# Sending the crossbar's q transpose two slots sooner in an attention and feed-forward kernel

The kernel runs on **one core of one Trainium2 chip**. The metric is the device time of one execution in microseconds (us), lower is better; medians of several runs are given with their range.

## The reference

```python
scale  = 1.0 / np.sqrt(64)                          # q, k, v: (8, 8, 576, 64) float32
scores = scale * np.matmul(q, k.transpose(0, 1, 3, 2))
thresh = np.max(scores, axis=-1, keepdims=True) - tau        # tau = 0.02
scores = np.where(scores >= thresh, scores, -1e9)
attn   = softmax(scores)                            # max taken off, sum + 1e-9
x = np.matmul(attn, v).transpose(0, 2, 1, 3).reshape(4608, 512)
h = x @ w_in                                        # 512 x 2048
y = (h - np.tanh(h)) @ w_out                        # 2048 x 512
```

## The kernel before

The 64 heads are handled as 32 **pairs**, 0 to 31. Each pair has nine score tiles; one tile is one **slot** of the schedule, and the scores run AHEAD = 8 slots in front of the rest. I write 9.5 for tile 5 of pair 9. Between the slots the program does the feed-forward layers of batches that are ready, so TensorE has work nearly all the time. The profiler's short names are used below: PE for TensorE's matmuls, PEld for its weight loads, DVE for VectorE, ACT for ScalarE, POOL for GpSimd, SPq for the sync engine's queue; L370 is line 370 of the kernel.

What a pair needs before its first tile is planned in slots ahead of it (cut to what matters):

```python
raw_pool = pool("raw", 2); hl_pool = pool("hl", 2); qk_pool = pool("qk", 2)
z_pool = pool("z", 4); zt_pool = pool("zt", 6); p_pool = pool("p", 3)

PREP = (
    (LDK, lambda p: load(p, "k")),          # LDK = 16; two DMAs each, sync queue
    (LDK - 1, lambda p: load(p, "q")),
    (LDK - 2, lambda p: load(p, "v")),
    (8, lambda p: split(p, "k")),           # GpSimd: float32 -> two fp16 halves
    (7, lambda p: split(p, "q")),
    (5, lambda p: turn(p, "k")),            # PE transposes, DVE copy
    (4, split_v),
)
for p in range(1, NPAIR):
    first = TPP * p - AHEAD
    for d, f in PREP[3 if p == 1 else 0 :]:
        d -= p == 1 and d in (3, 5)
        if d == 5 and p >= 5:
            d = 6 if p % 2 else 3
        plan.setdefault(first - d, []).append(lambda p=p, f=f: f(p))
    d = 5 if q_by_dma(p) else (2) if p >= 5 else 3 - (p == 1)
    plan.setdefault(first - d, []).append(lambda p=p: turn(p, "q"))
```

In 13 pairs (9, 11, ... 29, and 30 and 31) q is turned by the DMA crossbar, on the sync engine's queue; in the others by nine PE transposes and a DVE copy:

```python
def q_by_dma(p):
    return p >= 2 * HPAIR and (p % 2 == 1 or p == 30)

def turn(p, t):
    hl = hls.pop((p, t))
    if t == "q" and q_by_dma(p):
        m = mats[p, t] = qk_pool.tile([P, W], FP16, name=f"{t}T", tag=t)
        nc.sync.dma_start_transpose(out=..., in_=...)        # L247, qT<-qhl
        return
    ... # PE transposes to ps_q (L235), then nc.vector.tensor_copy (L258)
```

The same queue carries all loads, the output stores and 117 other transposes, one for most pairs of score tiles: ACT writes z, the crossbar turns it into zT, ACT takes the exponential of it (pT), and PE multiplies pT by v.

```python
def kink(i):        # ACT: z (L363)
    ...
        zts[i] = zt_pool.tile([P, TPP, P], BF16, name="zT")
        nc.sync.dma_start_transpose(out=zts[i], in_=zt)      # L370, zT<-z
def weights(i):     # ACT: pT = exp(zT) (L399); PE then uses pT (L420, L427)
```

## Time and profile before

| | before |
|---|---|
| median of 3 runs | 535.39 us (534.58 to 536.02) |
| profiled run | 536.14 us, span 534.4 us, granted clock 1.0 |

The prediction shows the engine table, the stretch from 100 to 440 us, the waits and one stall. Four more views are needed later. First pair 9, as the windows view has it from 115 to 130 us (its columns are window, length, busy us of PE, PEld, DVE, ACT, POOL, clock, DMA share and GB/s). ACT is busy 14.44 of 15 us here, against 307 of 340 over the whole stage:

```profile
115.00:130.00 15.00, 14.04 (x145) 7.91 (x142) 12.86 (x40) 14.44 (x20) 9.05 (x14) 1.00 1.02 201
```

### The profile page before, as it was taken

To read this page: it belongs to the slowest core of one execution; us is meant where nothing else is said; L and a number is where in the kernel's file an instruction comes from. 1 tells how busy PE (TensorE), PEld (TensorE's weight loads), DVE (VectorE), ACT (ScalarE), POOL (GpSimd) and SP (SyncE) were. 2 spreads that over 40 slices of the span, in tenths; PEclk is the share of its full clock that TensorE was granted. 3 is DMA by queue.
4 is the path that set the end of the run, shared out by engine and by line. 5 is a ranking of instruction groups with operands and counts; after the bars stand their busy time and mean duration, and the time that the engine had idled before them with its cause. 6 is when DMAs were issued, how large, how long until landed. Compare 5 with 4: busy or idle time off the path is not lost.

```text
span 534.4 us, 12822 instructions
## 1 busy us (share of the span) xinstructions
PE 509.6 (95%) x4651; PEld 289.2 (54%) x4651; DVE 423.3 (79%) x1184; ACT 436.7 (82%) x617; POOL 289.5 (54%) x390
## 2 busy tenths in 40 slices
PE   8988899999999998989999999999999999999997
PEld 4666566555555554555555555655555555444444
DVE  5888878989989897889889898899889887554440
ACT  5999899999898988899888989899889999543330
POOL 7999987775737566574727474575747530000000
PEclk9999999999999999999999999999999999999999
DMA  7655547999996999799998999798988995401113
GB/s 203 183 186 146 182 151 186 211 163 200 173 201 146 173 189 201 151 182 195 173 199 140 213 165 210 153 188 185 207 167 178 204 148 110 104 20 41 39 40 79
DMA packets 202687, 85.32 MB, mean 160 GB/s; under 512 B 170240, under 2 KB 195072, under 8 KB 202624
## 3 DMA queue, kind: packets, MB, share of 16 engines
q1 hardware_dynamic: 202032, 84.08, 75.2%
q8 instruction: 36, 0.59, 0.5%
q10 hardware_dynamic: 592, 0.43, 0.3%
q14 instruction: 27, 0.22, 0.1%
HBM read 36.70 MB, written 9.44 MB: 86 GB/s over the span
## 4 chain that ended last, share of the span: by engine, by line
PE 64%; DVE 9%; POOL 9%; DMA 7%; ACT 6%; issue 4%; SPq 0%; POOLq 0%; ACTq 0%; DVEq 0%
PE psY L519 20%; PE psH L493 16%; PE psS L326 14%; DMA qT<-qhl 5%; PE psO L427 3%; PE psHt L493 3%; DVE sc L336 3%; DVE g L512 2%; ACT z L363 2%; POOL kS L264 2%; PE psS L317 2%; DVE yo L532 2%; PE ps_k L235 2%; ACT th L506 1%; POOL w_in_sb L626 1%
## 5 line engine op out<-in xcount | busy, mean ns | idle before, releaser
L336 DVE TENSOR_SCALAR_CACHE_REDUCE sc<-psS 128x576 f32<-128x576 f32 x288 | 214.3, 752 | 40.7 <-PE psS L326 22.0
L363 ACT ACTIVATE z<-sc,nb 128x576 bf16<-128x576 f32 x288 | 217.2, 770 | 32.5 <-DVE nb L348 30.2
L519 PE MATMUL psY<-w_out_sb,g 128*128 128x512 bf16 (+1 forms) x592 | 145.9, 374 | 0.8 <-DVE yo L532 0.8
L264 POOL COPY kS<-kT 64x1152 f16<-64x1152 f16 x62 | 70.8, 1142 | 126.3 <-DVE nb L348 124.7
L399 ACT ACTIVATE pT<-zT 128x1152 f16<-128x1152 bf16 x117 | 135.0, 1154 | 2.0 <-DMA zT<-z 2.0
L493 PE MATMUL psH<-xT,w_in_sb 128*128 128x512 bf16 x480 | 123.3, 379 | 2.3 <-DVE g L512 2.3
L326 PE MATMUL psS<-kT,qT 128*128 128x512 f16 (+1 forms) x512 | 104.4, 285 | 4.6 <-DVE qT L258 1.2
L326 PEld LDWEIGHTS <-qT 128*128 128x128 f16 x1024 | 74.2, 97 | 59.2 <-issue 5.1
L512 DVE SCALAR_TENSOR_TENSOR g<-th,psH 128x512 bf16<-128x512 f32 x128 | 87.4, 683 | 18.9 <-ACT th L506 18.6
L326 PE MATMUL psS<-kS,qT 128*128 128x512 f16 x496 | 101.4, 286 | 0.0
L506 ACT ACTIVATE th<-psH 128x512 f32<-128x512 f32 x128 | 74.7, 583 | 23.7 <-PE psH L493 23.0
L519 PEld LDWEIGHTS <-g 128*128 128x128 bf16 x592 | 51.0, 98 | 56.8 <-issue 2.4
L493 PEld LDWEIGHTS <-w_in_sb 128*128 128x128 bf16 x576 | 49.1, 98 | 57.0 <-issue 4.7
L427 PE MATMUL psO<-vb,pT 128*128 128x65 bf16 x1024 | 53.3, 194 | 0.0
L427 PEld LDWEIGHTS <-pT 128*128 128x128 f16 x1024 | 44.2, 98 | 9.7
L188 POOL TENSOR_TENSOR qhl<-qraw,qhl 128x576 f16<-128x576 f32 x31 | 39.7, 1280 | 2.6
L188 POOL TENSOR_TENSOR khl<-kraw,khl 128x576 f16<-128x576 f32 x31 | 39.7, 1280 | 2.6
L391 ACT ACTIVATE pT<-psZ 128x512 f16<-128x512 bf16 (+1 forms) x54 | 35.0, 651 | 5.0 <-PE psZ L382 4.5
L532 DVE COPY yo<-psY 128x512 f32<-128x512 f32 (+1 forms) x31 | 21.1, 681 | 14.1 <-PE psY L519 12.4
L453 DVE TENSOR_TENSOR osb<-psO,rc 128x256 bf16<-128x256 f32 x64 | 27.1, 424 | 2.2
L420 PE MATMUL psO<-vb,pT 128*128 128x130 bf16 x128 | 28.2, 220 | 0.4
L258 DVE COPY kT<-ps_k 128x1152 f16<-128x1152 f16 x31 | 23.3, 752 | 5.8 <-PE ps_k L235 5.8
(79 smaller groups left out, 516.9 us busy)
## 6 DMA issues: line engine op xcount, KB each, us to landing
vraw<-in_v_dram SPq DMA_DIRECT2D x32, 256.0 KB, 3.7
out_dram<-yo SPq DMA_DIRECT2D x32, 256.0 KB, 3.1
kraw<-in_k_dram SPq DMA_DIRECT2D x31, 256.0 KB, 3.6
qraw<-in_q_dram SPq DMA_DIRECT2D x31, 256.0 KB, 3.7
wt<-in_moe_w_in_dram SPq DMA_DIRECT2D x8, 512.0 KB, 4.7
wt<-in_moe_w_out_dram SPq DMA_DIRECT2D x8, 512.0 KB, 4.4
zT<-z SPq DMA_TRANSPOSE x117, 3.5
kraw<-in_k_dram SPq DMA_DIRECT2D x32, 32.0 KB, 3.5
```

The lines of the kernel that those rows point to most:

```text
L188: nc.gpsimd.tensor_tensor(out=hl[:, :, 1, :], in0=x, in1=hl[:, :, 0, :], op=ALU.subtract)
L264: nc.gpsimd.tensor_copy(out=o, in_=i)
L326: nc.tensor.matmul(out=ps[:, dst], lhsT=lhs, rhs=kk[:, src], start=(n == 0), stop=(n == 1),)
L336: nc.vector.tensor_scalar(out=sc, in0=ps[:, lo : lo + S], scalar1=SC, scalar2=None, op0=ALU.mult, op1=ALU.max, accum_out=mx[:, c : c + 1],)
L363: nc.scalar.activation(out=z, in_=sc, func=ACT.Prelu, bias=nb, scale=1.0, alpha=STEEP)
L391: nc.scalar.activation(out=pt[:, off * P : (off + n) * P], in_=ps[:, 0 : n * P], func=ACT.Exp)
L399: nc.scalar.activation(out=pt[:, 0 : n * P], in_=zts.pop(i)[:, 0:n, :], func=ACT.Exp)
L427: nc.tensor.matmul(out=po[:, t - 1 + ab, :], lhsT=pt[:, blk * P : (blk + 1) * P], rhs=vb[:, hh, c, :], start=False, stop=(n == 7), skip_gr ...
L493: nc.tensor.matmul(out=ps, lhsT=w_in_sb[:, c, n * P : (n + 1) * P], rhs=xs[m][:, c, :] if m < B else xR[:, c, :, :], start=(c == 0), stop= ...
L506: nc.scalar.activation(out=th, in_=ps, func=ACT.Tanh)
L512: nc.vector.scalar_tensor_tensor(out=gs[m][:, n, :], in0=th, scalar=-1.0, in1=ps, op0=ALU.mult, op1=ALU.add,)
L519: nc.tensor.matmul(out=ps, lhsT=gs[m][:, n, ms * P : (ms + 1) * P], rhs=w_out_sb[:, n, cols], start=(n == 0), stop=(n == DF_C - 1),)
```

## The change

The intent: the q transpose leaves the queue earlier, so that PE need not wait for it at the first tile of a pair. For that GpSimd's split of k and q is planned two slots sooner too. And pairs 2 and 4, still turned by PE, turn q one slot later.

```diff
@@ -654,10 +654,12 @@
         for d, f in PREP[3 if p == 1 else 0 :]:
             d -= p == 1 and d in (3, 5)
+            if d in (7, 8) and q_by_dma(p):
+                d = d + 2
             if d == 5 and p >= 5:
                 d = 6 if p % 2 else 3
             plan.setdefault(first - d, []).append(lambda p=p, f=f: f(p))
-        d = 5 if q_by_dma(p) else (2) if p >= 5 else 3 - (p == 1)
+        d = 7 if q_by_dma(p) else 3 - (p == 1 or p % 2 == 0 or p >= 5)
         plan.setdefault(first - d, []).append(lambda p=p: turn(p, "q"))
```

## The prediction

> **What bounds the kernel now.** I read the page's engine table first, then the stretch in which attention and the two feed-forward layers run together, then the list of waits, then the chain of waits, then the timeline around one stall. The engine table, and the busy time of each engine from 100 to 440 us (columns: window, length, busy us of PE, PEld, DVE, ACT, POOL with instruction counts, clock, DMA share, GB/s):
>
> ```profile
> PE 509.6 (95%) x4651; PEld 289.2 (54%) x4651; DVE 423.3 (79%) x1184; ACT 436.7 (82%) x617; POOL 289.5 (54%) x390
> ```
>
> ```profile
> 100.00:440.00 340.00, 331.53 (x3070) 187.05 (x3067) 297.97 (x847) 306.97 (x413) 201.59 (x259) 1.00 0.94 180
> ```
>
> TensorE is busy 331.5 of 340 us there; ACT has 10% to spare, DVE 12%, POOL 41%, and the clock is granted in full. So only something that idles PE can be won: at most 340 - 331.5 = 8.5 us by that row. The last 70 us are feed-forward layers alone, which the change does not touch. What idles PE is in the list of waits (engine, line, what it waited for: us in total, times, longest):
>
> ```profile
> PEld L317 <- DMA qT<-qhl: 7.3, 8, 1.7
> ...
> PE psS L317 <- DMA qT<-qhl: 3.4, 3, 1.4
> ...
> PEld L326 <- DMA qT<-qhl: 1.0, 1, 1.0
> ...
> PE psS L326 <- DMA qT<-qhl: 0.9, 1, 0.9
> ```
>
> The greatest wait of PE by far is for the crossbar-turned q of a new pair. The matmul rows are the same events as some of the weight rows, seen one pipeline stage later, so they must not be added. The chain of waits around 231 us (start, length, what):
>
> ```profile
> 230.60 0.06 POOL kS L264
> 230.66 1.06 issue
> 231.72 5.72 DMA qT<-qhl
> 237.44 0.04 issue
> 237.48 0.69 PE psS L317 x8
> ```
>
> The transfer sent at 231.72 lands at 237.44 and PE goes on 0.04 us later. The timeline of the same stretch shows why it was sent no sooner (start, length, instruction):
>
> ```profile
> 226.13 1.30 SPq L370 DMA_TRANSPOSE zT<-z  x1
> ...
> 226.38 1.28 POOL L188 TENSOR_TENSOR qhl<-qraw,qhl 128x576 f16<-128x576 f32 x1
> ...
> 227.53 0.53 SPq L145 DMA_DIRECT2D kraw<-in_k_dram  x1
> ...
> 230.35 1.26 SPq L370 DMA_TRANSPOSE zT<-z  x1
> ...
> 231.72 2.02 SPq L247 DMA_TRANSPOSE qT<-qhl  x1
> ...
> 237.48 0.39 PEld L317 LDWEIGHTS <-qT 128*64 128x64 f16 x8 [1.73 <-DMA qT<-qhl]
> ```
>
> GpSimd had the split q ready at 226.38 + 1.28 = 227.66, 4.1 us before the transfer left. Between the two the sync queue sent four loads and a zT, because the program puts them ahead.
>
> **What the skill says.** (1) The Trainium skill, "Perfetto Trace Analysis", section "Per-instruction lifecycle: what the profiler-reported window actually captures": a hardware-queue DMA's slice covers the issuing and not the movement. The trace agrees: the issue at 231.72 took 2.02 us, its landing 5.72 us. So I take landings from the chain and from semaphores. (2) "DMA: Bandwidth & Descriptors", section "Queues, rings and completion order": all DMAs of the sync engine share one ring on each of the 16 DMA engines, consumed in ring order. Sending q sooner therefore makes what it overtakes later. The trace agrees in kind: in the back-to-back stretch from 227.53 us zT took 6.2 us to land, against 3.5 in the median. (3) The first page's section "Identifying the Most-Contended Engine" calls matmul busy time a bad measure of headroom because matmuls are pipelined. Here PEld is at 54% while PE is at 95%, so I size the gain from the gaps in front of single weight loads, not from the 95%.
>
> **The change part by part.** The order of instructions on each engine, compared between the two builds, shows how little really moves.
>
> Splitting two slots sooner: GpSimd's sequence is identical in both kernels, so this part only lets the sync queue's instruction follow in program order. Gain by itself: 0.
>
> Sending two slots sooner: 13 transfers (pairs 9, 11, ... 29, and 30, 31). In the usual case one jumps over four loads, sometimes an output store, and one zT. From transfer to transfer (231.72, 260.49, 290.69) two pairs, 18 slots, take about 29 us, so a slot is 1.62 us and two are 3.2 us. It can use nearly all of that: by the trace the split was ready 3.9 to 5.9 us before the old issue in all 13 cases. In the new place the sync queue reaches the transfer within about 0.2 us of the split's end (227.48 against 227.66 in the case shown; the same offset in most pairs), so the queue hardly blocks. The longest wait, 1.73 us, is less than 3.2 us: all these waits should vanish.
>
> Size: the weight-load rows give 7.3 + 1.0 = 8.3 us in 9 events. A load after such a change of tile costs some 0.23 us in any case (the timeline shows [0.23 <-issue] in front of the next group at 238.10), so 9 x 0.23 = 2.1 us stays, and 6.2 us goes. Taking the excess of start-to-start distances of matmuls over their usual distance I get 6.2 us too, in seven pairs (9, 15, 17, 19, 21, 30 at 0.3 to 1.6 us each, one negligible); in the other six q came in time already. Nearly all of it is on the path, as PE sets the pace of this stage.
>
> Given back: the zT that is overtaken leaves one transposing issue later (1.3 to 2.7 us). Most of these zT lie ready 1.6 to 3.4 us before ACT reads them, but in pairs 9, 15 and 17 only 1.24, 0.58 and 0.66 us. I count 1 us of ACT waiting in each of these three, 3 us, and a third of it passed on to PE, since ACT has 10% to spare and the result is used two slots later: 1 us.
>
> Pairs 2 and 4 turn q (nine PE transposes) one tile later, and the DVE copy of 0.75 us moves behind the next bias. There the list of waits has PE waiting for DVE's qT copy 1.2 us in 2 events; in those stretches ACT runs without a gap, so the wait is mostly not the path. I count 0, give or take 0.3 us.
>
> Sum: 535.4 - 6.2 + 1.0 = **530.2 us**, 1.0% faster.
>
> **The rivals.** (a) *The wait moves to zT.* If the crossbar, not the place in the queue, is scarce (DMA share 0.94 over this stage), the overtaken zT land where q landed before, ACT waits in more pairs, and th and z behind it are late. For it: landings of 6.2 us when two transposes queue behind four loads, and a zT with a slack of 0.1 us right after the transfer in four pairs. Against it: ACT waited for zT only 2.0 us (4 times) in all, and zT's median slack is 3.2 us. It would give back 3 to 6 us: 532 to 535. (b) *ACT or DVE becomes the bound.* PE's stalls let ACT catch up; in some 15 us windows ACT is busy 14.8. With the stalls gone ACT's share rises from 307/340 to 307/334 = 92%, so a lasting bound is unlikely, but PE may wait more for g and for psS. It would leave 2 to 3 us of gain: 532 to 533. (c) *The sync queue blocks.* If GpSimd is late, the transfer holds up zT and loads behind it. The split is ready within 0.2 us in most pairs (0.6 in pair 9), and loads are sent a whole pair ahead, so this costs under 0.5 us. (d) *More than the stalls.* If a stall also delays the chain behind it (DVE waited 1.35 us at 238.21 for the same q), removing it gains no more than PE lost; 8.5 us is the ceiling: 527.
>
> **Range and chances.** The sum gives 530.2. Rivals (a) and (b) pull towards 533, the ceiling towards 528; runs before spread from 534.6 to 536.0. I take 528.2 to 533.4 as 8 in 10. Faster by over 2% means under 524.7, more than the whole idle time of PE in the stage: 2%. Slower by over 2% would need the sync queue to jam: 1%. Within 2%: 97%.
>
> **What would show it.** Right: the waits of PE and PEld for DMA qT fall from 8.3 us to under 1; q is sent about 3 us sooner (near 228 in the case shown) and lands before 234; PE's idle time from 100 to 440 us falls by about 5 us; GpSimd's busy time stays. The give-back is seen in ACT's wait for zT: 2.0 us now, 3 to 5 expected. Wrong: PEld still waits for qT (then the DMA, not the place in the queue, is slow); ACT pT waiting for zT beyond 6 us with new PE waits for pT or g (rival a); PE idle as before with DVE or ACT as the releasers (rival b); the sync queue waiting long for GpSimd's qhl (rival c).

## More of the kernel before

Third, the waits of ACT for zT and of PE for pT (total, times, longest), both small:

```profile
ACT pT L399 <- DMA zT<-z: 2.0, 4, 0.9
...
PEld L420 <- ACT pT L399: 1.3, 3, 0.4
```

Fourth, a line of the queue table that looks like nothing (packets, MB, share). It is TensorE's instruction stream, in 36 packets of 16,384 bytes; one such packet is called a fetch below:

```profile
q8 instruction: 36, 0.59, 0.5%
```

Second, the sync queue's timeline in pair 9 (start, length, instruction). The four loads of k and q have gone out by 114.4; then come a zT, the q transpose, the v loads and three zT:

```profile
114.44 1.84 SPq L370 DMA_TRANSPOSE zT<-z  x1
116.46 1.31 SPq L247 DMA_TRANSPOSE qT<-qhl  x1
117.83 0.62 SPq L145 DMA_DIRECT2D vraw<-in_v_dram  x1
118.49 0.66 SPq L151 DMA_DIRECT2D vraw<-in_v_dram  x1
119.25 4.40 SPq L370 DMA_TRANSPOSE zT<-z  x3
```

## The result

| | before | after |
|---|---|---|
| median, range | 535.62 us, 534.58 to 536.02 (4 runs) | **533.94 us**, 533.65 to 534.50 (4 runs) |
| ratio | | 0.9973, 95% interval 0.9956 to 0.9990 |
| profiled run, span | 536.14, 534.4 us | 534.50, 532.5 us |

All these runs are at clock 1.0. A ratio is the mean time of one kernel's fast runs over the mean of the other's of the same rounds, so it is not quite the ratio of the medians. The change is real and small: about 1.5 us of the 5.2 predicted, and outside the predicted range.

**The wait that was to go is gone.** In the list of waits of the kernel after, no line has PE or PEld waiting for DMA qT; before they were 8.3 us. The case that the prediction shows, near 231 us, reads now (sync queue):

```profile
226.16 1.30 SPq L370 DMA_TRANSPOSE zT<-z  x1
227.73 1.30 SPq L247 DMA_TRANSPOSE qT<-qhl  x1
229.09 0.58 SPq L145 DMA_DIRECT2D kraw<-in_k_dram  x1
...
231.59 1.84 SPq L370 DMA_TRANSPOSE zT<-z  x1
```

The transfer leaves at 227.73 instead of 231.72 and lands at 230.97. PE first loads from it at 235.89, in the second half of the 16 loads of L317 that begin at 235.40.

**Other waits have grown.** The list of waits of the kernel after, for the same two pairs of names as above, with one new line (PE for pT) and what the sync queue itself waited for GpSimd:

```profile
PEld L420 <- ACT pT L399: 4.5, 8, 1.0
...
ACT pT L399 <- DMA zT<-z: 3.7, 6, 1.4
...
PE psO L420 <- ACT pT L399: 1.1, 2, 0.6
```

```profile
SPq L247 <- POOL qhl L188: 2.3, 10, 0.5
```

ACT waits 1.7 us more for zT and PE's weight loads 3.2 us more for pT. ACT's longest such waits after are 1.48 us in two pieces in pair 9, where there was none before, and 1.45 near 425 us (0.46 before). The timeline of pair 9 shows how it comes about. The q transpose now goes ahead of the four loads. The zT, which stands behind the loads as before, leaves at 116.91 instead of 114.44:

```profile
113.06 1.28 SPq L247 DMA_TRANSPOSE qT<-qhl  x1
114.39 0.58 SPq L145 DMA_DIRECT2D kraw<-in_k_dram  x1
115.02 0.56 SPq L153 DMA_DIRECT2D kraw<-in_k_dram  x1
115.63 0.59 SPq L145 DMA_DIRECT2D qraw<-in_q_dram  x1
116.27 0.55 SPq L153 DMA_DIRECT2D qraw<-in_q_dram  x1
116.91 1.83 SPq L370 DMA_TRANSPOSE zT<-z  x1
118.79 0.59 SPq L145 DMA_DIRECT2D vraw<-in_v_dram  x1
119.43 0.65 SPq L151 DMA_DIRECT2D vraw<-in_v_dram  x1
120.18 5.03 SPq L370 DMA_TRANSPOSE zT<-z  x3
```

The queue issues without a pause for 12 us. ACT and PE in the same stretch (brackets: idle time before, and what ended it):

```profile
120.95 1.16 ACT L399 ACTIVATE pT<-zT 128x1152 f16<-128x1152 bf16 x1 [0.50 <-DMA zT<-z]
...
122.17 0.10 PEld L420 LDWEIGHTS <-pT 128*128 128x128 f16 x1 [0.76 <-ACT pT L399]
...
124.43 1.16 ACT L399 ACTIVATE pT<-zT 128x1152 f16<-128x1152 bf16 x1 [0.98 <-DMA zT<-z]
...
125.64 0.10 PEld L420 LDWEIGHTS <-pT 128*128 128x128 f16 x1 [0.53 <-ACT pT L399]
```

Two zT come late in a row, and PE waits after each of them. In the chain of waits of the kernel before, this stretch ran through PE's and DVE's own work. After, it hangs on the crossbar:

```profile
116.91 7.42 DMA zT<-z x2
```

In the 15 us window DVE and ACT now get less done (ACT 14.44 us before, 13.51 after) although their instructions are the same:

```profile
115.00:130.00 15.00, 14.22 (x143) 7.83 (x143) 12.34 (x39) 13.51 (x18) 9.64 (x14) 1.00 0.90 192
```

The PE column can't be compared: this trace lacks 67 matmul records (4584 instead of 4651), and gaps of about 217 ns beside psH and psY, the feed-forward matmuls, are missing records.

**A ledger.** To see where time comes and goes without PE's records, I took the start of each of the 288 score evictions by DVE (L336, one per tile) in each trace, and subtracted its start in the first profile of before. Between events the difference stays constant to 0.01 us, so a step in it is a gain or a loss of the whole pipeline. For the kernel after, the gains are −0.94 us at 9.0, −1.31 at pair 15, −1.43 at 17, −0.17 at 19, −0.70 at 21 and −0.56 at 30: **−5.1 us**. The losses are +0.44 before the first tile, +0.15 in the early pairs, **+1.69 in tiles 9.1 to 10.0** (the greatest step, +1.19, at 9.5), +0.30 in 17, +0.58 in 21 and +0.17 in 30: **+3.3 us**. The end comes 1.84 us sooner.

### The profile page after: what moved, and what is told of

Read it like the earlier page. It is cut to its first block, busy times and chain, and to the rows that moved or that the text cites. A ratio compares the mean times of both kernels' runs of the same rounds, so it can differ in the third digit from the quotient of the medians.

```text
span 532.5 us, 12733 instructions
## 1 busy us (share of the span) xinstructions
PE 505.7 (95%) x4584; PEld 289.0 (54%) x4651; DVE 424.0 (80%) x1184; ACT 436.0 (82%) x617; POOL 290.3 (55%) x390
## 4 chain that ended last, share of the span: by engine, by line
PE 62%; ACT 11%; POOL 9%; DVE 8%; issue 5%; DMA 4%; SPq 0%; POOLq 0%; ACTq 0%; DVEq 0%
PE psY L519 20%; PE psH L493 16%; PE psS L326 13%; ACT z L363 5%; DMA zT<-z 3%; PE psO L427 3%; ACT pT L399 3%; PE psHt L493 3%; DVE sc L336 3%; POOL kS L264 2%; ACT th L506 2%; DVE g L512 2%; PE ps_k L235 2%; PE psS L317 2%; POOL w_in_sb L626 1%
## 5 line engine op out<-in xcount | busy, mean ns | idle before, releaser
L336 DVE TENSOR_SCALAR_CACHE_REDUCE sc<-psS 128x576 f32<-128x576 f32 x288 | 214.3, 753 | 36.8 <-PE psS L326 22.8
L519 PE MATMUL psY<-w_out_sb,g 128*128 128x512 bf16 (+1 forms) x571 | 141.7, 373 | 2.4 <-issue 0.8
L493 PE MATMUL psH<-xT,w_in_sb 128*128 128x512 bf16 x436 | 114.1, 379 | 4.3 <-DVE g L512 2.3
```

Of the source, the lines that this page charges most:

```text
L336: nc.vector.tensor_scalar(out=sc, in0=ps[:, lo : lo + S], scalar1=SC, scalar2=None, op0=ALU.mult, op1=ALU.max, accum_out=mx[:, c : c + 1],)
L493: nc.tensor.matmul(out=ps, lhsT=w_in_sb[:, c, n * P : (n + 1) * P], rhs=xs[m][:, c, :] if m < B else xR[:, c, :, :], start=(c == 0), stop= ...
L519: nc.tensor.matmul(out=ps, lhsT=gs[m][:, n, ms * P : (ms + 1) * P], rhs=w_out_sb[:, n, cols], start=(n == 0), stop=(n == DF_C - 1),)
```

## The experiments

**Theory.** The transfer sent sooner wins its waits, but in pair 9 it makes one unbroken stretch on the sync queue with the loads of the next pair; the zT behind come late, ACT has no slack there and passes the delay on to PE. **Rivals.** (1) The splits, planned sooner, disturb GpSimd or DVE. (2) The early pairs' part costs the time. (3) The profile of before was an unlucky sample: its waits are not what an average run has. (4) TensorE's instruction fetches, which the profile counts on the same 16 DMA engines, decide which transfers are late.

The times first; "before" is the kernel before in the same job. All results were correct.

| run | job | us, median | before, median | ratio to before, 95% |
|---|---|---|---|---|
| split_back | 1 | 533.78 | 534.84 | 0.9982, 0.9963 to 1.0002 |
| early_back | 1 | 533.41 | 534.84 | 0.9977, 0.9957 to 0.9997 |
| loads_early | 1 | 531.90 | 534.84 | 0.9945, 0.9921 to 0.9969 |
| late_start | 1 | 533.89 | 534.84 | 0.9981, 0.9960 to 1.0001 |
| loads_early_only | 2 | 534.10 | 534.71 | 0.9993, 0.9975 to 1.0012 |
| shift_fetch | 2 | 535.38 | 534.71 | 1.0022, 1.0001 to 1.0044 |
| rep_before, rep_before2 | 2 | 533.88, 533.31 | 534.71 | single runs |
| late_and_early_back | 3 | 533.20 | 534.42 | 0.9978, 0.9956 to 1.0000 |
| loads_early_best | 3 | **531.58** | 534.42 | 0.9948, 0.9931 to 0.9966 |
| one_slot | 3 | 532.65 | 534.42 | 0.9966, 0.9941 to 0.9991 |
| shift_fetch_after | 3 | 533.13 | 534.42 | 0.9974, 0.9951 to 0.9997 |
| before_fetch28 | 4 | 535.68 | 535.03 | 1.0024, 0.9993 to 1.0054 |
| after_fetch100 | 4 | 536.40 | 535.03 | 1.0021, 0.9980 to 1.0061 |

And the ledger of every trace, as steps in us over stretches of pairs (first column: where it stands at the end of pair 7; the steps add up to the last column):

| trace | to pair 7 | 8 to 10 | 11 to 16 | 17 to 20 | 21 to 31 | end |
|---|---|---|---|---|---|---|
| before, first profile | 0 | 0 | 0 | 0 | 0 | 0 |
| rep_before | −0.43 | −0.04 | −0.58 | −0.72 | −0.50 | −2.27 |
| rep_before2 | −0.34 | +0.14 | −1.27 | −0.90 | −0.47 | −2.84 |
| after | +0.56 | +0.78 | −1.31 | −1.31 | −0.56 | −1.84 |
| split_back | +0.77 | +0.59 | −1.43 | −1.31 | −1.20 | −2.58 |
| early_back | +0.44 | +1.01 | −1.46 | −1.32 | −0.92 | −2.25 |
| late_start | +0.51 | +1.12 | −1.59 | −1.31 | −0.76 | −2.03 |
| loads_early | +0.36 | −0.51 | −1.60 | −1.32 | −1.20 | −4.27 |
| loads_early_only | +0.11 | −0.88 | −0.65 | +0.01 | −0.61 | −2.02 |
| shift_fetch | −0.16 | +1.15 | −1.59 | −1.32 | −0.65 | −2.57 |
| late_and_early_back | +0.40 | −0.04 | −1.60 | −1.32 | −0.98 | −3.54 |
| loads_early_best | +0.23 | −0.91 | −1.59 | −1.32 | −0.95 | −4.54 |
| one_slot | +0.28 | +0.94 | −1.27 | −1.33 | −0.53 | −1.91 |
| shift_fetch_after | +0.01 | +0.54 | −1.49 | −1.32 | −1.13 | −3.39 |
| before_fetch28 | +0.03 | +1.04 | −0.38 | −1.30 | −0.14 | −0.75 |
| after_fetch100 | +2.16 | +1.75 | −1.37 | −1.31 | −0.59 | +0.64 |

One profile is one run, so the ends differ from the medians; the stretches tell more. From pair 11 to 20 every kernel with the change gains 2.6 to 2.9 us on the first profile of before, 1.31 to 1.33 of it in pairs 17 to 20. That is no measure of the change by itself: shift_fetch, in the old order, gains 2.9 there too, and the other two profiles of before 1.3 and 2.2.

**split_back**: the change with the splits in their old slots.

```diff
-            if d in (7, 8) and q_by_dma(p):
-                d = d + 2
```

> The changed kernel with the splits left in their old slots (transfer still two slots sooner). The order of instructions and their waits is the same as in the changed kernel on every engine, so it also serves as a second profile of it. Theory (the earlier split does nothing, and the loss at pair 9 is a steady thing of this order of the sync queue): time within 0.5 us of the changed kernel's 533.9; in the ledger of score tiles against the kernel before, pair 9 again gains about 0.9 us and then loses about 1.6, pair 15 and 17 gain 1.3 and 1.4. Rival (pair 9's loss and the 0.44 us at the start are chance of one execution): pair 9 ends with a gain, or the start differs by another amount.

The compiled kernel has the same order of instructions and waits on every engine as the change. Time 533.78 us; the ledger has the gains of the change and the loss in pairs 8 to 10. In pair 9 ACT waited 0.38 and 0.92 us for zT, and 1.50 us were lost after tile 9.0. So the split part does nothing, rival 1 falls, and this run is a repeat of the kernel after: the 0.58 us lost in pair 21 of the first trace are not in this one, so they are chance, while the losses of pairs 9 and 17 come again.

**early_back**: pairs 2 and 4 turn q as before.

```diff
-        d = 7 if q_by_dma(p) else 3 - (p == 1 or p % 2 == 0 or p >= 5)
+        d = 7 if q_by_dma(p) else (2) if p >= 5 else 3 - (p == 1)
```

> The changed kernel with pairs 2 and 4 turning q in their old slot. In the ledger the score tiles of pairs 1 to 4 lost 0.08 us at each of the two turns. Theory: the loss of 0.08 + 0.05 us goes, the rest of the ledger stays, time 0.1 to 0.2 us lower than the changed kernel, not visible in the median. Rival (the early turns set up the loss at pair 9 by shifting what comes later): pair 9 no longer loses 1.6 us, and the time falls by over 1 us, to about 532.5.

533.41 us, 0.4 less than split_back in the same job, from which it differs in this and in the inert splits. Two other pairs of runs agree in sign (late_start 533.89 and late_and_early_back 533.20; loads_early 531.90 and loads_early_best 531.58), though these lie in different jobs and the intervals overlap. The early part costs a few tenths at most; it isn't the missing 3.7 us, so rival 2 explains little.

**loads_early**: the change, and the loads of even pairs from 10 on are sent four slots sooner, so that they are out of the stretch.

```diff
             if d in (7, 8) and q_by_dma(p):
                 d = d + 2
+            if d in (LDK, LDK - 1, LDK - 2) and p % 2 == 0 and p >= 10:
+                d = d + 4
```

> The changed kernel with the loads of k, q and v of even pairs from 10 on sent four slots sooner, so that they leave in the idle time of the sync queue before the transfer of q and not between it and the zT behind it. Theory (the gain is given back because transfer, four to six loads and the zT behind them leave one sync queue back to back, so that zT comes late to ACT in pairs 9, 21 and 30): ACT's wait for zT falls from 3.7 us to under 1.5 us, pairs 9, 21 and 30 keep their gains of 0.9, 0.7 and 0.6 us, time 531 to 532. Rival (with q in time ACT or DVE is the bound, or PE's order behind the new pair is): the give-backs stay, time 533.5 to 534.5. Second rival (DMA bandwidth, not the queue's order, is scarce): zT waits move to other pairs and the time stays within 0.5 us of 533.9.

531.90 us, 1.9 less than split_back in the same job. ACT waits for no zT in pair 9. The ledger shows where: against split_back it gains 1.1 us in pairs 8 to 10 (+0.59 there, −0.51 here), 0.4 before pair 8, 0.17 in 11 to 16, and nothing after. Behind pair 16 its steps equal split_back's to 0.01 us. This is what the theory asks for, and it places the cost in pair 9.

**late_start**: the change from pair 11 on, pair 9 as before.

```diff
-            if d in (7, 8) and q_by_dma(p):
+            if d in (7, 8) and q_by_dma(p) and p >= 11:
-        d = 7 if q_by_dma(p) else ...
+        d = (7 if p >= 11 else 5) if q_by_dma(p) else ...
```

> The changed kernel with pair 9, the first whose q is turned by the crossbar, left as before (split and transfer in their old slots); pairs from 11 on as changed. In the ledger pair 9 went from +0.56 to +1.34 us, a net loss of 0.78 us. Theory: this pair alone accounts for it, so the time falls by 0.8 us, to about 533.1, and the rest of the ledger keeps its steps (15: -1.3, 17: -1.4 and +0.3, 21: -0.7 and +0.6). Rival (the loss comes at the first crossbar pair, whichever it is, as a kind of filling up of the queue): the loss moves to pair 11 and the time stays at 533.9.

533.89 us. The theory in its simple form asked for before's pair 9; instead 1.12 us were lost in pairs 8 to 10, in the old order. In its list of waits one q wait is left, that of pair 9:

```profile
PEld L317 <- DMA qT<-qhl: 1.1, 1, 1.1
```

The two waits for zT in ACT's list lie elsewhere, but the list has this line too, and it is of pair 9:

```profile
ACT pT L399 <- PE psH L493: 1.5, 1, 1.5
```

It is a wait for zT all the same, put down to the matmul whose event came last. The zT that this pT reads left at 119.64, behind the v loads, and landed at 124.61; pT began 0.10 us later, as after each of the other late zT of pair 9. (split_back's 0.92 us stands under psH too.) So a late zT is the cause here as well, in the old order, and a fetch was in flight with it. That led to the packets of queue 8 (rival 4).

**rep_before, rep_before2**: the kernel before, unchanged, profiled twice more.

> The kernel before, profiled a second time, to see what of the ledger is chance of its one profile. In late_start pair 9 was sent as before and still lost 1.1 us in its sixth tile, as the changed kernel does. Theory A (the first profile of the kernel before was lucky at pair 9: the 16 KB instruction fetch fell at 123.7 us, after the tight stretch, where the other profiles have it at 120 to 121 us inside it): the second profile shows the sixth tile of pair 9 about 1.1 us later than the first, or its fetch again at another time. Theory B (the loss is given back by the change): the second profile agrees with the first at pair 9 within 0.2 us. The start of the first score tile, 8.39 us in the first profile and 8.7 to 9.0 in all others, should be 8.4 if it belongs to the kernel and above 8.6 if it is chance.

> The kernel before, profiled a third time; same expectations as for rep_before. Timed runs of the kernel before spread from 533.3 to 536.0 us, so theory A also expects the three profiles to differ by over 1 us in span, in steps at pairs where a fetch falls into a transfer.

Each is a single run, 533.88 and 533.31 us. Their waits of PE's weight loads for q:

```profile
PEld L317 <- DMA qT<-qhl: 6.7, 10, 1.4
```

```profile
PEld L317 <- DMA qT<-qhl: 4.7, 7, 1.3
```

By the ledger's measure, the time from the last tile of the old pair to the first of the new one less the same time in the kernel after, the waits for q cost 5.1, 3.8 and 2.8 us in the three profiles of before, **3.9 in the mean**. (The expectation of one_slot has 4.8 for this mean, by distances of matmuls; that figure could not be worked out again from the traces.) The wait of pair 15 was 1.7, 1.4 and 0.0 us; that of pair 9 stayed (1.2, 1.2, 1.3). The profiled run that I sized from, 536.14 us, lies at the top of the 533.11 to 536.29 us which the kernel before took over all jobs. So rival 3 holds in part.

**shift_fetch, shift_fetch_after, before_fetch28, after_fetch100**: 64, 28 or 100 one-column matmuls added to the warm-up, before any data has landed, in the kernel before or after. They move TensorE's fetches against the pairs; nothing else in the program is changed, though the first tile comes at another time, too (−0.1 to +2.7 us).

```diff
     for n in range(11):
         nc.tensor.matmul(out=pz, lhsT=zero[:, 0:P], rhs=zero, start=True, stop=True)
+    for n in range(64):
+        nc.tensor.matmul(out=pz[:, 0:1], lhsT=zero[:, 0:P], rhs=zero[:, 0:1], start=True, stop=True)
```

> The kernel before with 64 one-column warm-up matmuls added at the start, before any data is there, so that every later TensorE instruction lies 128 places later in its stream and the 16 KB fetches (256 instructions) fall about 7 us, half a pair, sooner against the work. Theory (q comes late in pairs 15, 17, 19 and 21 because a fetch holds one DMA engine for 1 to 2 us while the transfer is in flight): these waits vanish or fall under 0.5 us in sum; waits show instead, if at all, at other pairs, where the shifted fetch meets the transfer. Rival (the order of the sync queue alone makes q late): the waits of pairs 15 and 17 stay at 1.3 to 1.4 us. The start may be later by up to 3 us for the added matmuls, which says nothing.

> The changed kernel with the 64 added one-column warm-up matmuls of shift_fetch, to be compared with it (same chip differences aside, by the ledger). Theory (the give-back at pair 9 is the fetch falling into the back-to-back stretch of the sync queue): the fetch now falls at about 113 and 127 us, and the sixth tile of pair 9 does not lose 1.1 us, in contrast to the changed kernel; against shift_fetch the step at the start of pair 9 is a gain of up to 2 us (its wait for q was 2.3 us), all waits for q are gone, and the time is 2 to 3 us under shift_fetch's 535.4. Rival (the give-back belongs to the order of the queue alone): the loss of 1.1 us at pair 9's sixth tile is there.

> The kernel before with 28 one-column warm-up matmuls added at the start, so that the fetch that falls 1286 weight loads in (no loss at pair 9, four profiles of four) should fall about 1258 loads into the real work, where all kernels with the loss at pair 9 have it. Theory (the place of this fetch makes the loss): pair 9's sixth tile comes about 1.1 us later than in the profiles of the kernel before, though nothing of the change is in this kernel; the time is not lower than the kernel before's. Rival (the loss comes from the change): no step above 0.3 us at pair 9's sixth tile.

> The changed kernel with 100 one-column warm-up matmuls added, which moves the fetches 28 loads later against the work (128 - 100), so that the one at pair 9 falls near 1286. Theory: pair 9 keeps its gain of 0.9 us and its sixth tile does not lose 1.1; no PE wait for q; the first tiles start up to 3 us later for the added matmuls, part of it caught up by pair 2. Rival (the order of the sync queue alone makes the loss): the loss of 1.1 us at pair 9's sixth tile stays.

A fetch comes once in some 128 weight loads with their 128 matmuls, about every 14.0 us; a pair takes 14.6 us. So the fetch drifts slowly through the pairs. Over nine traces (the three of before, the change, split_back, early_back, loads_early, late_start, one_slot) I sorted the crossbar transposes by whether a fetch was in flight between issue and landing:

| | transposes | median to landing | over 4.3 us |
|---|---|---|---|
| fetch in flight | 389 | 4.5 us | 225 |
| none | 781 | 3.4 us | 14 |

A longer transfer is likelier to meet a fetch. But sorted by whether a fetch began within 3 us of the issue, which doesn't depend on the transfer's length, the medians are 4.6 and 3.4 us, so this bias isn't the reason. With the fetches moved the waits move. In shift_fetch, the old order, the q waits of 15, 19 and 21 are gone, and pair 9 waits 2.3 us; in before_fetch28 pairs 9, 11, 13 and 30 wait (2.2, 1.5, 0.7, 1.4) and 17 and 21 don't:

```profile
PEld L319 <- DMA qT<-qhl: 4.1, 4, 2.3
```

```profile
PEld L319 <- DMA qT<-qhl: 5.7, 6, 2.2
```

(The edit shifts the line numbers by two.) So the waits of pairs 15 to 21 go with the fetch. In the three profiles of before, too, a fetch was in flight with each of these transfers except that of pair 15 in rep_before2, whose wait was 0.0. The fetch does not decide all: pairs 9 and 30 waited in all three profiles, 0.8 to 1.3 us, with no fetch in flight. The kernel itself isn't helped by either: 1.0022 and 1.0024. (Both profiles are of the fastest of the four runs; shift_fetch's other three took 535.34 to 536.21 us against 533.57.) The 28 matmuls were meant to put the fetch of pair 9 where the change has it, near 1,258 weight loads; it fell at 1,222 and hit the q transfer itself. after_fetch100 also began its tiles 2.71 us late, of which 2.16 were left at the end of pair 7, so its total says nothing; only its steps are used.

For pair 9 these runs also settle less than I had hoped. Where the fetch falls, in us from the last tile of pair 8, and the step over pairs 8 to 10:

| order in pair 9 | fetch, step |
|---|---|
| old | +4.7: 0 (before); +4.6: −0.04; +4.8: +0.14; +4.8: −0.04; +1.8: +1.12; −1.2: +1.04; −5.7: +1.15 |
| changed | +0.5: +0.78 (after); +0.9: +0.59; +0.6: +1.01; +0.2: +0.94; −5.8: +0.54; +3.9: +1.75 |
| old, loads out | +1.4: −0.88 |
| changed, loads out | +0.8: −0.51; +0.6: −0.91 |

The old order loses 1.1 us as soon as the fetch leaves its lucky place, but not always in the same way: with the fetch at +1.8 by the late zT, with it at −1.2 and −5.7 by a longer wait for q (2.2 and 2.3 us), all of it at tile 9.0; the changed order brings no gain with any of the three places; with the loads out of the stretch both gain 0.5 to 0.9, with the fetch in one of the places that cost the others. I had expected of after_fetch100 that a fetch late in the stretch would free the changed order. Its fetch hit a zT behind, ACT waited 2.1 us, and that form of the theory fell.

What goes with the loss behind tile 9.0 in all sixteen traces is a late zT. This is ACT's idle time in pair 9 that ended with the landing of the zT it was to read, beside what the ledger lost from tile 9.1 to 10.0:

| | ACT waits for zT | lost |
|---|---|---|
| after | 1.48 | 1.69 |
| split_back | 1.30 | 1.50 |
| early_back | 0.95 | 1.27 |
| late_start | 1.47 | 1.24 |
| one_slot | 1.76 | 1.85 |
| shift_fetch_after | 1.24 | 1.44 |
| after_fetch100 | 2.46 | 2.66 |
| the nine others | 0 | 0.0 |

In shift_fetch_after no fetch was in flight with either late zT; the nearest, which met the q transfer, ended 2.4 us before the first of them left. So the changed order can make the loss without a fetch on a late zT; in late_start the old order makes it with one.

**loads_early_only**: the kernel before with the loads sooner, the transfer in its old place.

> The kernel before with only the loads of even pairs from 10 on sent four slots sooner, transfer of q in its old slot. Theory (the transfer was late because four loads stand ahead of it, and zT behind it late for the same reason): most of the 6.2 us of waits for q vanish without moving the transfer, since it no longer queues behind the loads: time 531 to 532.5, within 0.7 us of loads_early. Rival (only the transfer's own two slots help): waits for q stay above 4 us and the time within 1 us of the kernel before.

534.10 us, 0.9993. Pair 9 gains 0.88, but in pair 19, which waits 1.6 us for q, nearly 1 us is lost, and the waits for q of 15 and 17 are partly there. Alone it is worth about nothing; on top of the change, 0.9945 against 0.9982. **The two parts help each other.**

**late_and_early_back**: late_start and early_back in one; instructions as before up to pair 11.

> Pairs 2 and 4 turn q and pair 9 sends q as in the kernel before; only the transfers from pair 11 on leave two slots sooner. Up to pair 11 every engine has the instructions of the kernel before in the same order. In the three profiles of the kernel before, the tenth instruction fetch falls at 123.2 to 123.7 us (1286 weight loads in) and pair 9 loses nothing; in the changed kernel and in late_start it falls at 120.0 to 121.3 (1251 to 1260 loads in) and pair 9's sixth tile loses 1.1 us. Theory (the place of the fetch, not pair 9's own transfer, decides): if the fetch is again past 123 us, no loss at pair 9, and the time is near 532.5; if it falls at 120 to 121, the loss of 1.1 us comes although nothing before it was changed. Rival (the early pairs' later turn makes the loss): no loss here in either case, because those turns are back.

533.20 us. Here the fetch is at +4.8 as in before, and nothing is lost in pairs 8 to 10 (−0.04). In the eight other edited kernels without warm-up matmuls it came at +0.2 to +1.8. The early pairs, pair 9's own change and the loads are each enough to move it (late_start, early_back, loads_early_only); why is open.

**one_slot**: one slot instead of two (`d + 1` for the splits, `6 if q_by_dma(p)`).

> The changed kernel with splits and transfers one slot sooner instead of two. One slot is 1.6 us and the longest wait for q was 1.7 us, but the transfer still stands ahead of two loads and the zT. Theory: waits for q fall from about 4.8 us (mean of three profiles) to under 1 us, the zT behind is pushed back as before, time within 0.5 us of the changed kernel's 533.9. Rival (two slots are more than is needed and the push is what costs): time 533.0 or less.

Unclear. The median, 532.65 us, is lower than the change's, but the profiled run was its slowest (534.75), and in it pair 9 loses as much (+0.94). Whether one slot beats two isn't settled.

**loads_early_best**: loads_early with pairs 2 and 4 as before.

> Candidate for the best version: transfers two slots sooner, loads of even pairs four slots sooner, pairs 2 and 4 as before. Theory: as loads_early (531.9 us) less the 0.1 to 0.2 us of the early turns: 531.5 to 532.0, no PE wait for q, pair 9's sixth tile loses nothing. Rival (loads_early's gain was chance of one chip): time 533 or more.

**531.58 us (531.28 to 531.99, six runs), the fastest of all**, 2.8 under the median of before in its job. Its pair 9 on the sync queue: the stretch starts with the transfer and the next zT follows at once, with the k load behind:

```profile
114.10 1.32 SPq L247 DMA_TRANSPOSE qT<-qhl  x1
115.52 7.64 SPq L370 DMA_TRANSPOSE zT<-z  x4
123.21 0.58 SPq L145 DMA_DIRECT2D kraw<-in_k_dram  x1
```

ACT takes zT without a wait here (two waits, 1.9 us in all, are left elsewhere in the trace), and is busy in every moment of the window, PE in 14.93 of 15 us:

```profile
115.00:130.00 15.00, 14.93 (x152) 8.54 (x151) 13.64 (x44) 15.00 (x21) 9.62 (x15) 1.00 0.90 178
```

That ACT is at 15.00 of 15 us shows how little slack it has there.

## Why the prediction was wrong

The direction, and "within 2%", were right. The size was not: 1.4 to 1.7 us gained (ratio or medians; 1.1 in the repeat split_back) where 5.2 were predicted. Two terms of the sum failed, items 4 and 5.

1. **What bounds the kernel, and which wait goes: right.** PE was stopped by q in pairs 9, 15, 17, 19, 21 and 30, and these waits are gone in every trace with the change. The transfer near 228 us left and landed as predicted.
2. **The splits gain nothing by themselves: right**, shown by split_back.
3. **The queue hardly blocks on GpSimd: nearly right.** It waited 2.3 us in ten places, 0.5 at most, where under 0.5 in all was predicted. In pair 9 its 0.5 us is part of what pushed zT back, with the 1.28 us of the transfer's issue; no experiment separates the two.
4. **"6.2 us goes": the step that failed first, by its size.** The mechanism was right, but the figure came from one profile of a run at the top of the spread, and not all of PE's wait was on the path. By the ledger the waits cost 5.1 us in that profile and 3.8 and 2.8 in two more. On the mean of the three, 3.9, the term is 2.3 us too large.
5. **"I count 1 us of ACT waiting in each of these three, 3 us, and a third of it passed on to PE, since ACT has 10% to spare": the step that failed in its mechanism.** The late zT of pair 9 left 2.5 us later (116.91 against 114.44, of which 0.6 is the lateness of the whole pipeline there), inside the stated 1.3 to 2.7. ACT's wait for zT in all, 3.7 us, was also inside the stated 3 to 5. But ACT's 10% is an average over 340 us; in this window it had 0.56 of 15 us. It waited 0.50 + 0.98 = 1.48 us, and the pipeline lost 1.69: as much as the wait, not a third of it. So it was, to 0.3 us, in all seven traces with such a wait. The second wait, for the zT behind the v loads, wasn't in the sum, though rival (a) names such zT with 0.1 us of slack. What is passed on isn't a share of the wait but the wait less the slack of that place. Pair 30 shows it: ACT has 12.88 of 15 us busy there before (418 to 433 us). In the seven traces in which it waited 1.33 to 1.71 us for zT near 425 us, the loss at tile 30.4 was that wait less 1.28 us, to 0.01 us; of waits up to 1.10 us nothing was lost. In pairs 15 and 17, where I also expected late zT, ACT waited for none in this trace; the 0.30 us lost in 17 are in loads_early too, so they don't come from zT. The give-back by zT is thus in one pair and 1.7 us, with 0.2 in pair 30, instead of spread over three and 1.0.
6. **The early pairs, "0, give or take 0.3": about right**, 0.15 us by the ledger, 0.3 to 0.7 by medians which aren't sharp enough.
7. **Not thought of:** the first tile came 0.44 us later in the trace of after, 0.1 to 0.6 later in seven of the eight other edited kernels without warm-ups, and 1.0 sooner in one_slot, with the same instructions there; in the profiles it goes with which half of the first loads lands last. It is not explained. Nor did I see that a fetch of instructions takes part in the waits.

As an estimate from the ledger: 3.9 for the waits that went, less 1.7 in pair 9, 0.3 in 17, 0.2 in 30 and 0.15 in the early pairs, leaves some 1.6 us; less the 0.44 of the later first tile, 1.1. The measured gain lies between 1.1 and 1.7. So items 4 and 5 account for most of the shortfall, and the first is the larger: 2.3 us against 0.9.

Rival (a), the wait moving to zT, was the true one in kind, and its 532 to 535 us held the result. Its argument, that the crossbar is scarce, was not quite what the runs show: taking plain loads out of the stretch (k, q and v of the next pair) removes the loss, with as many transposes as before.

**Open:** how much of pair 9's loss in the kernel after is the new order and how much the fetch that moved with it. The changed order makes such a loss with no fetch on either late zT (shift_fetch_after, 1.44 us, though a fetch met the q transfer ahead of them), and a fetch can make it in the old order (late_start, 1.24). At a like place of the fetch the changed order is 0.1 to 0.6 us better than the old one (+0.2 to +0.9 against +1.8, and −5.8 against −5.7) or 1.75 worse (+3.9 against +4.7). What in a fetch slows another transfer isn't shown either. That the stretch of loads is needed for the loss is shown in both orders.

## What to carry to other kernels

A transfer that is sent sooner on a busy queue makes another one later: look up who reads the overtaken transfers and how much slack that reader has in that very window, not on average; in these traces a wait up to the slack cost nothing and what went beyond it was passed on (pair 30: 1.28 us of slack; pair 9: none). When the list of waits names an engine that had no reason to be late, compare the landing of the DMA: 0.9 to 1.5 us of waiting for zT stood under another name here. Take other issues out of the stretch in the same change; here the transfer alone gave 0.9973 and the loads alone 0.9993, both together 0.9945. And size a wait from several profiles, after looking where the profiled run lies in the spread of times.

## What the Trainium skill lacked or had wrong

- "Runtime: NRT & Kernel Launch", section "Instruction fetch mechanics": it gives blocks of 16 KiB, 256 instructions, and the runs agree (36 packets of 16,384 bytes, one per some 256 TensorE instructions). It calls the cost of crossing a block "one DMA tail-bump, mostly hidden". For the engine's own stream nothing here speaks against that, but the fetch isn't hidden from other transfers: crossbar transposes with one in flight landed in 4.5 us in the median against 3.4, and moving the fetches by 64 or 28 tiny matmuls took the waits for q away from pairs 17 and 21 and, with 28, brought them to 11 and 13.
- "DMA: Bandwidth & Descriptors" gives sequencer cycles for an SBUF-to-SBUF crossbar transpose of 8,192 tiles, in a table about a later chip, and no time that could be used for one of 128x1152 two-byte elements: in the kernel before it held the issuing queue 1.24 to 2.74 us, 1.35 in the median, against 0.56 for a k or q load. In the kernel after, five of them beside six loads filled the sync queue for 12 us.
- "Perfetto Trace Analysis", section "What 'DMA-bound' means", names the issuing engine's sequencer as one bound, and pair 9 agrees (12 us without a pause). It speaks of a kernel that is bound so; here it held for one pair, and the waits of the readers showed it, not a share of the span.
